# Router logits with the gate matrix as weights, and token rows of 320 columns

## The chip, the cores and the metric

The kernel runs on one core of a Trainium2 chip. The metric is the device time of one execution in microseconds (us), as the median of several runs. The core's engines are TensorE (PE, with its weight loads shown apart as PEld), VectorE (DVE), ScalarE (ACT), GpSimd (POOL) and SyncE (SP, which here only issues transfers).

## The reference

Three layers follow one another: a gated linear attention over 4 batches, 8 heads and 768 tokens, a router that gives each of the 3072 tokens to one of 8 experts with 384 tokens each, and a dense layer after the experts.

```python
def _moe_ref(x, w_gate, w1, w2):            # x: 3072 x 320, the attention's output
    logits = x @ w_gate                     # 320 x 8
    order = np.argsort(-logits.flatten())
    ...
    # in falling order: a token not yet placed goes to its expert while that has room (cap 384)
    for e in range(E):
        mask = assigned == e
        h = np.maximum(x[mask] @ w1[e], 0.0)    # 320 -> 1024
        out[mask] = h @ w2[e]                   # 1024 -> 320
    return out

def _moe2_ref(x, w_in, w_out):              # 320 -> 2048 -> 320
    h = x @ w_in
    g = np.where(h > 0.0, h, np.exp(np.minimum(h, 0.0)) - 1.0)
    return g @ w_out
```

## The kernel before

**Attention, about 0 to 168 us.** The work is cut into 24 units u: 12 blocks of 64 tokens by 2 pairs of batches, so that a unit has 128 tokens. `Attention.run` goes over the units. In one pass of its loop TensorE does, in this order: a zeroing matmul (L348), the values and scores (L357 and L289, 64x64 matmuls in f32), the decay matrices pD and pF (L314, L304, L307), the three transposes of the unit before (`turn(u-1)`, L428), recall and state (L371 and L384), and the logits of the unit before (L438). Meanwhile DVE divides and gates the unit's output into `x` (L404 to L411), POOL scales it (L412), ACT doubles its last 64 columns (L419) so that a row has 384 columns, and SP stores the rows to the scratch tensor `xd` in DRAM (L422). `turn` puts x^T into PSUM (`pX`), ACT copies it to `xT` (L430), and `logits` multiplies: xT is the weights (128 columns), and the 8 columns of the gate matrix `wg` move through it. ACT copies the 128x8 result to `L` (L439). Between the units, queues that were filled before (`at.extra`) give out other work: the first steps of the routing, four units at a time (`rt.early`, lines L610 to L630 on DVE), and the loading and splitting of weights (L872 to L938).

**Routing of the first expert, about 168 to 199 us.** A chain of small steps on DVE and TensorE selects the first 384 tokens.

**Eight rounds, about 199 to 768 us.** Each takes one expert's 384 tokens through the expert and then the dense layer. `get_x` gathers the rows of `xd` by indirect transfers of 128 rows each, issued by POOL (L996, tile `xg`). `prep_x` transposes them (`turn(k)`, three transposes for each of three tiles, L1061), and ACT and DVE split the result into two parts, xh and xl. The last 64 of the 320 columns are wanted twice, on partitions 0 to 63 and 64 to 127; in the kernel before the rows hold them twice. Then come the matmuls of the expert (L1108 with w1h, w1l; L1202 to L1217) and of the dense layer (L1108 with wih, wil; L1247 to L1251). Where the rounds' other work stands in TensorE's order is set by a planner with costs; the transposes of the next round stand among the dense layer's matmuls of the round before.

Of the kernel before, what the change touches and what calls it, by code (L numbers as in the profile page):

```python
# [8 lines left out]
F32 = mybir.dt.float32  # L9
# [3 lines left out]
AF = mybir.ActivationFunctionType  # L13
# [3 lines left out]
B, H, S, D = 4, 8, 768, 40  # L17
# [11 lines left out]
EP = [0, 1, 1, 1, 1, 1]  # L29
FU = 1  # L30
SPIN, IDLE, MX = 12, 1, [256, 512, 640]
NB, NL, PX = 2, 3, 0.2
WARM = [8, 2, 2, 2]

# [84 lines left out]
class Attention:  # L119
# [4 lines left out]
    def __init__(self, nc, tc, consts, qk, vk, ig, fg, wg, xd, L, ident):  # L124
        self.nc, self.tc, self.qk, self.vk, self.xd, self.L, self.ident = nc, tc, qk, vk, xd, L, ident
        self.es = ExitStack()
        one = self.es.enter_context(tc.tile_pool(name="a1", bufs=1))
        self.two = self.es.enter_context(tc.tile_pool(name="a2", bufs=2))
        self.psX = self.es.enter_context(tc.tile_pool(name="psX", bufs=1, space=PS))
        V, G, A = nc.vector, nc.gpsimd, nc.scalar  # L130
# [24 lines left out]
            self.load_vk(u)  # L155
        for u in range(2, 4):
            self.load_qk(u)
        self.wg = one.tile([128, 3, 8], F32, name="wg")
        nc.sync.dma_start(self.wg, wg)
        for u in range(2, 4):  # L160
            self.load_vk(u)
        m = one.tile([32, S + 1], F32, name="m")
        V.memset(m[:, 0:1], -1e30)
        keep = one.tile([32, S], F32, name="keep")
        G.memset(keep, 1.0)
        G.memset(keep[:, 0:S:64], 0.0)
        ac = one.tile([32, S], F32, name="ac")
# [27 lines left out]
        for x in self.KT:  # L195
            G.memset(x, 0.0)
        self.pC = self.psum("pC", 1)
        self.g = gi, gf, m, keep, ac

        t0, t1 = slice(0, 128), slice(128, S)  # L200
# [7 lines left out]
        self.decay(0)  # L208
        self.maximum(128, S)
        V.memset(self.pC, 0.0)  # L210
        self.decay(1)
        self.both(self.scores(1))
        self.weigh(0)
        self.fade(0)
        self.logs(2, NS)

    def psum(self, name, bufs):
        return self.psX.tile([128, 8, 64], F32, name=name, bufs=bufs)
# [180 lines left out]
    def gates(self, u, fl):  # L399

        V = self.nc.vector
        nq = self.st["O", u][:, :, 40]
        rd = self.two.tile([128, 2, 8], F32, name="rd")
        V.tensor_scalar(rd[:, 0], nq, -2.0, 2.0, op0=ALU.mult, op1=ALU.max)  # L404
        fl(1)
        V.scalar_tensor_tensor(rd[:, 0], nq, 2.0, rd[:, 0], op0=ALU.mult, op1=ALU.max)
        fl(5)
        V.reciprocal(rd[:, 1], rd[:, 0])
        x = self.st["x", u] = self.two.tile([128, 384], F32, name="x", bufs=3)
        xh = x[:, :320].rearrange("p (h d) -> p h d", d=40)  # L410
        V.scalar_tensor_tensor(xh, self.st.pop(("sg", u)), 1.0, self.st.pop(("O", u))[:, :, :40], op0=ALU.add, op1=ALU.mult)  # L411
        self.nc.gpsimd.tensor_tensor(xh, xh, rd[:, 1, :, None].to_broadcast([128, 8, 40]), op=ALU.mult)  # L412

    def rows_out(self, u):

        nc = self.nc
        n, bp = divmod(u, 2)
        x = self.st["x", u]
        nc.scalar.activation(x[:, 320:], x[:, 256:320], AF.Copy)  # L419
        for r in range(2):  # L420
            row = (bp * 2 + 1 - r) * S + n * 64
            nc.sync.dma_start(self.xd[row:row + 64], x[r * 64:r * 64 + 64])  # L422

    def turn(self, u):
        x = self.st.pop(("x", u))
        p = self.st["T", u] = self.psum("pX", 1).rearrange("p h t -> p (h t)")
        for k in range(3):
            self.nc.tensor.transpose(p[:, k * 128:k * 128 + 128], x[:, k * 128:k * 128 + 128], self.ident)  # L428
        xT = self.st["xT", u] = self.two.tile([128, 3, 128], F32, name="xT")
        self.nc.scalar.activation(xT.rearrange("p k t -> p (k t)"), p[:, :384], AF.Copy)  # L430

    def logits(self, u):

        l = self.st.pop(("T", u))[:, 384:392]
        x = self.st.pop(("xT", u))
        for k in range(3):
            z = 128 if k < 2 else 64
            self.nc.tensor.matmul(l, x[:z, k], self.wg[:z, k], start=k == 0, stop=k == 2)  # L438
        self.nc.scalar.activation(self.L[:, :, u % 4 * 6 + u // 4], l, AF.Copy)  # L439

    def step(self):

# [3 lines left out]
    def run(self, hook, fill):  # L446
        later = self.split(2, NS)
        for u in range(NU):
            v, w = u + 1, u + 2
            fl = lambda i: ([fill() for _ in range(FP[i])] if u > FU else []) + [self.step() for _ in range(EP[i])]  # L450
            self.idle(u)
            self.both(self.values(u), self.scores(w))
            if u < 3:
                next(later, None)
            if w < NU:
                self.decay(w)
            if u > 0:
                self.turn(u - 1)
            self.both(self.recall(u), self.state(u))
            if v < NU:  # L460
                self.factors(v)
                self.weigh(v)
            if u + 5 < NU:
                self.load_qk(u + 5)
            if v < NU:
                self.opens(v)
            fl(0)
            if v < NU:
                self.fade(v)
            self.gates(u, fl)  # L470
            fl(2)
            if u > 0:
                self.logits(u - 1)
            self.add_state(u)
            fl(3)
            if u == NU - 1:
                while self.extra:
                    self.step()
            self.rows_out(u)
            if u + 4 < NU:  # L480
                self.load_vk(u + 4)
            fl(4)
            hook(u)
        self.turn(u)
        self.logits(u)
        hook(NU)
        self.es.close()
# [336 lines left out]
class Mlp:  # L824
# [209 lines left out]
    def get_x(self, r):  # L1034
        idx = self.router.res[r][1]
        self.xg = []
        for k in range(3):
            t = self.pool.tile([128, 384], F32, name="xg", bufs=3)
            self.xg.append(t)
            self.gather(t, self.xd, idx[:, k:k + 1])  # L1040

# [10 lines left out]
    def prep_x(self, r):  # L1052

        nc, plan = self.nc, self.plan
        xh = self.pool.tile([128, 3, TK], F32R, name="xh", bufs=1)
        xl = self.pool.tile([128, 3, TK], F32R, name="xl", bufs=1)
        ps = []

        def turn(k):
            for t in range(3):  # L1060
                nc.tensor.transpose(ps[k][0][:, t * 128:t * 128 + 128], self.xg[k][:, t * 128:t * 128 + 128], self.ident)  # L1061

        def split(k):
            p, slot = ps[k]
# [17 lines left out]
        if r == 0:  # L1082
            ps = [self.psum() for t in range(3)]
# [336 lines left out]
def kernel(ctx, tc, qk, vk, ig, fg, wg, w1a, w1b, w2a, win, wout, out):  # L1420
    nc = tc.nc
# [4 lines left out]
    ident = consts.tile([128, 128], F32, name="ident")  # L1426
    make_identity(nc, ident)
    L = consts.tile([128, 8, 24], F32, name="L")
    xd = dram.tile([3072, 384], F32, name="xd")
    rt = Router.__new__(Router)  # L1430
    plan = Plan()
    m = Mlp(nc, tc, consts, w1a, w1b, w2a, win, wout, xd, out, ident, rt, plan)
# [13 lines left out]
    def hook(u):  # L1446
        if u in (0, 1):
            fill()
        if u == 2:
            at.extra.append(tables)  # L1450
        if 4 <= u < 23 and u % 4 == 0:
            at.extra.append(rt.early(u // 4 - 1))
        if u == 22:
            at.extra.append(rt.early(5, 0, 2))
        if u == 23:
            at.extra.append(rt.early(5, 2, 3))
        if u == 24:
            while at.extra:
                at.step()
            rt.dg = rt.digits(0)  # L1460
            for _ in rt.early(5, 3, 4, rt.dg):
                pass
# [9 lines left out]
    ps = ctx.enter_context(tc.tile_pool(name="ps", bufs=NPH, space=PS))  # L1472
# [8 lines left out]
def _layout(i):  # L1481
# [22 lines left out]
    d["ig"], d["fg"] = (i[n].reshape(2, 2, 8, 768).swapaxes(0, 1).reshape(32, 768) for n in ("i_gate", "f_gate"))  # L1504
    wg = i["moe_w_gate"][:, ::-1]
    d["wg"] = np.concatenate([wg, np.zeros((64, 8), wg.dtype)]).reshape(3, 128, 8).transpose(1, 0, 2)
    d["w1a"] = i["moe_w1"][:, :256].reshape(2048, 1024)
    d["w1b"] = i["moe_w1"][:, 256:].reshape(512, 1024)
    d["w2a"] = i["moe_w2"].reshape(8, 2, 4, 128, 320).transpose(0, 1, 3, 2, 4).reshape(2048, 1280)
# [20 lines left out]
```

## Time and profile before

| | us |
|---|---|
| time, median of 3 runs | 777.46 (776.14 to 778.16) |
| profiled execution | 777.53 |
| its span, first to last instruction | 775.5 |
| TensorE busy | 714.9 (92%) |
| VectorE busy | 543.0 (70%) |
| ScalarE busy | 383.0 (49%) |
| GpSimd busy | 214.5 (28%) |

The profile is of one execution. Its own time is 2.0 us longer than its span. A step of TensorE is best read from one start to the next, since matmuls are pipelined and the durations of neighbours overlap. The granted clock of TensorE is given as a share of full speed: 1.00 is 2.4 GHz, 0.50 is 1.2 GHz.

### The profile page before, as it was taken

To read this page: it belongs to the slowest core of one execution; us is meant where nothing else is said; L and a number is where in the kernel's file an instruction comes from. 1 tells how busy PE (TensorE), PEld (TensorE's weight loads), DVE (VectorE), ACT (ScalarE), POOL (GpSimd) and SP (SyncE) were. 2 spreads that over 40 slices of the span, in tenths; PEclk is the share of its full clock that TensorE was granted. 3 is DMA by queue.
4 is the path that set the end of the run, shared out by engine and by line. 5 is a ranking of instruction groups with operands and counts; after the bars stand their busy time and mean duration, and the time that the engine had idled before them with its cause. 6 is when DMAs were issued, how large, how long until landed. Compare 5 with 4: busy or idle time off the path is not lost.

```text
span 775.5 us, 18282 instructions
## 1 busy us (share of the span) xinstructions
PE 714.9 (92%) x7375; PEld 659.9 (85%) x7379; DVE 543.0 (70%) x1599; ACT 383.0 (49%) x817; POOL 214.5 (28%) x264
## 2 busy tenths in 40 slices
PE   7889787971899999999999999999999999999994
PEld 4767576861799998999999899999999999999994
DVE  8486787658878887885797589669868834842541
ACT  5655544433536644662575277246527734742541
POOL 5677767425411320301121031112023230001001
PEclk9699998685799999999999999999999999999998
DMA  7677967433500410310140032023003321100000
GB/s 256 193 227 214 247 198 215 138 94 94 181 8 1 146 61 2 118 64 27 26 156 19 9 102 79 26 83 99 1 26 108 130 77 39 35 1 27 0 1 26
DMA packets 22820, 68.86 MB, mean 89 GB/s; under 512 B 3536, under 2 KB 7632, under 8 KB 22736
## 3 DMA queue, kind: packets, MB, share of 16 engines
q1 hardware_dynamic: 14240, 35.87, 15.7%
q0 software_dynamic: 8448, 31.73, 12.6%
q8 instruction: 58, 0.95, 0.5%
q14 instruction: 26, 0.21, 0.1%
q10 hardware_dynamic: 48, 0.10, 0.0%
HBM read 59.03 MB, written 8.65 MB: 87 GB/s over the span
## 4 chain that ended last, share of the span: by engine, by line
PE 64%; issue 18%; DVE 8%; POOL 3%; ACT 3%; DMA 2%; SPq 0%; POOLq 0%; DVEq 0%; ACTq 0%
PE ph L1108 26%; PE acc L1247 5%; PE acc L1251 5%; PE acc L1248 5%; PE acc L1215 3%; PE acc L1217 2%; PE acc L1216 2%; PE pO L371 2%; PE pO L357 2%; PE pX L438 2%; DMA vk<-in_vk_dram 1%; PE acc L1202 1%; PE acc L1204 1%; PE pX L428 1%; DVE e L1161 1%
## 5 line engine op out<-in xcount | busy, mean ns | idle before, releaser
L1161 DVE SCALAR_TENSOR_TENSOR e<-e,ph 128x384 f32<-128x384 f32 x128 | 70.4, 550 | 54.7 <-ACT e L1158 54.1
L1157 ACT ACTIVATE e<-ph 128x384 f32<-128x384 f32 x128 | 62.4, 487 | 85.3 <-PE ph L1108 77.7
L1108 PE MATMUL ph<-yh,wih 128*128 128x384 f32 x256 | 89.9, 351 | 0.3
L1125 ACT ACTIVATE gh<-ph 128x384 fp32r<-128x384 f32 x64 | 31.4, 491 | 113.0 <-PE ph L1108 88.8
L1108 PE MATMUL ph<-yh,wil 128*128 128x384 f32 x256 | 86.6, 338 | 0.0
L1257 POOL DMA_INDIRECT out_dram<-ot,idx x24 | 24.1, 1004 | 210.1 <-ACT ot L985 207.1
L992 DVE TENSOR_TENSOR gl<-e,gh 128x384 fp32r<-128x384 f32 x128 | 71.0, 561 | 1.7 <-ACT gh L985 0.3
L1158 ACT ACTIVATE e<-e 128x384 f32<-128x384 f32 x128 | 67.3, 526 | 4.0
L1132 DVE SCALAR_TENSOR_TENSOR gl<-ph,gh 128x384 fp32r<-128x384 f32 x64 | 35.3, 554 | 46.9 <-ACT gh L1125 46.5
L1247 PE MATMUL acc<-woh,gh 128*128 128x320 f32 x216 | 68.1, 315 | 0.0
L1248 PE MATMUL acc<-wol,gh 128*128 128x320 f32 x216 | 66.7, 309 | 0.0
L1251 PE MATMUL acc<-woh,gl 128*128 128x320 f32 x216 | 66.7, 309 | 0.0
L1108 PE MATMUL ph<-yl,wih 128*128 128x384 f32 x256 | 66.6, 341 | 0.0
L996 POOL DMA_INDIRECT stg<-in_w1a_dram,wi x16 | 15.7, 982 | 148.6 <-DVE wi L765 134.2
L985 ACT ACTIVATE gh<-e 128x384 fp32r<-128x384 f32 x97 | 49.4, 514 | 11.1 <-DVE e L1161 10.8
L1251 PE MATMUL acc<-woa,gl 128*128 128x320 f32 x168 | 52.4, 312 | 0.8 <-DVE gl L992 0.8
L1247 PE MATMUL acc<-woa,gh 128*128 128x320 f32 x168 | 53.1, 316 | 0.0
L1248 PE MATMUL acc<-wob,gh 128*128 128x320 f32 x168 | 51.9, 309 | 0.0
L1108 PEld LDWEIGHTS ph<-yh,wih 128*128 128x128 f32 x256 | 48.2, 188 | 4.1 <-ACT yh L1220 4.1
L1108 PEld LDWEIGHTS ph<-yh,wil 128*128 128x128 f32 x256 | 48.1, 188 | 0.0
L1108 PEld LDWEIGHTS ph<-yl,wih 128*128 128x128 f32 x256 | 46.2, 188 | 0.0
L1108 PE MATMUL ph<-xh,w1h 128*128 128x384 f32 x128 | 44.9, 351 | 0.1
(269 smaller groups left out, 2118.2 us busy)
## 6 DMA issues: line engine op xcount, KB each, us to landing
vk<-in_vk_dram SPq DMA_DIRECT2D x24, 484.0 KB, 4.5
qk<-in_qk_dram SPq DMA_DIRECT2D x20, 320.0 KB, 5.3
xd<-x SPq DMA_DIRECT2D x48, 96.0 KB, 2.6
cx<-in_win_dram SPq DMA_DIRECT2D x8, 512.0 KB, 5.5
wx<-in_wout_dram SPq DMA_DIRECT2D x9, 320.0 KB, 3.1
cx<-in_wout_dram SPq DMA_DIRECT2D x5, 448.0 KB, 6.2
qk<-in_qk_dram SPq DMA_DIRECT2D x4, 512.0 KB, 7.2
cx<-in_win_dram SPq DMA_DIRECT2D x4, 256.0 KB, 7.4
```

The lines of the kernel that those rows point to most:

```text
L985: self.nc.scalar.activation(out, x, AF.Copy)
L992: self.nc.vector.tensor_tensor(out, x, y, op=ALU.subtract)
L1108: PE.matmul(p, w, x, start=k == 0, stop=k == 7)
L1125: nc.scalar.activation(h, p, AF.Relu)
L1132: nc.vector.scalar_tensor_tensor(l, p, 0.0, h, op0=ALU.max, op1=ALU.subtract)
L1157: nc.scalar.activation(e, p, AF.Relu, scale=-1.0)
L1158: nc.scalar.activation(e, e, AF.Exp, scale=-1.0)
L1161: nc.vector.scalar_tensor_tensor(e, e, -1.0, p, op0=ALU.add, op1=ALU.max)
L1247: PE.matmul(p, h[:, c], wh, start=f == 0, stop=False)
L1248: PE.matmul(p, h[:, c], wl, start=False, stop=False)
L1251: PE.matmul(p, l[:, c], wh, start=False, stop=f == 15)
L1257: s = nc.gpsimd.indirect_dma_start(out=self.out, out_offset=bass.IndirectOffsetOnAxis(ap=idx[:, t:t + 1], axis=0), in_=o, in_offset=None)
```

## The change

For units 0 to 19 (`TG = 20`) the logits change sides: the gate matrix, padded from 8 to 32 columns, is the weights, and the 128 columns of xT move. The result is 32 rows (8 of them used) by 128 tokens, and the four units of a group stand on the four quarters of the partitions of one PSUM tile. After four units one ACT copy takes that tile to `lT` in SBUF, and one unit later `tokens(g)` transposes it back on TensorE and copies 128x32 values into `L`. Units 20 to 23 keep the old form. `pX` is now one fixed PSUM tile that is zeroed once on DVE. `wg` lies in a part of the tile `keep` and is loaded after the scans that read `keep`. The early steps of the routing come one unit later (units 5, 9, ..., 21).

Rows of `x`, `xd` and `xg` have 320 columns, and ACT's copy of the last 64 is gone. In the attention the third transpose takes 64 columns. In the rounds the third transpose is replaced by two f32 matmuls with the 64 columns as weights and the identity moving, one to partitions 0 to 63 and one to 64 to 127.

```diff
+TG = 20
...
-        self.wg = one.tile([128, 3, 8], F32, name="wg")
-        nc.sync.dma_start(self.wg, wg)
...
-        keep = one.tile([32, S], F32, name="keep")
+        keep = keep_all = one.tile([128, S], F32, name="keep")
+        self.lT, keep = keep[:, :128], keep[:32]
+        self.wg = keep_all[:, 128:224].rearrange("p (k e) -> p k e", e=32)
...
+        self.pX = self.psum("pX", 1).rearrange("p h t -> p (h t)")
...
+        V.memset(self.pX, 0.0)
...
         self.logs(2, NS)
+        nc.sync.dma_start(self.wg, wg)
...
-        nc.scalar.activation(x[:, 320:], x[:, 256:320], AF.Copy)
...
-        p = self.st["T", u] = self.psum("pX", 1).rearrange("p h t -> p (h t)")
+        p = self.pX
         for k in range(3):
-            self.nc.tensor.transpose(p[:, k * 128:k * 128 + 128], x[:, k * 128:k * 128 + 128], self.ident)
+            z = 128 if k < 2 else 64
+            self.nc.tensor.transpose(p[:z, k * 128:k * 128 + 128], x[:, k * 128:k * 128 + z], self.ident)
...
     def logits(self, u):
-        l = self.st.pop(("T", u))[:, 384:392]
         x = self.st.pop(("xT", u))
+        b = u % 4 * 32
+        l = self.pX[:, 384:392] if u >= TG else self.pX[b:b + 32, 384:512]
         for k in range(3):
             z = 128 if k < 2 else 64
-            self.nc.tensor.matmul(l, x[:z, k], self.wg[:z, k], start=k == 0, stop=k == 2)
-        self.nc.scalar.activation(self.L[:, :, u % 4 * 6 + u // 4], l, AF.Copy)
+            if u >= TG:
+                self.nc.tensor.matmul(l, x[:z, k], self.wg[:z, k, :8], start=k == 0, stop=k == 2)
+            else:
+                self.nc.tensor.matmul(l, self.wg[:z, k], x[:z, k], start=k == 0, stop=k == 2)
+        if u >= TG:
+            self.nc.scalar.activation(self.L[:, :, u % 4 * 6 + u // 4], l, AF.Copy)
+        elif u % 4 == 3:
+            self.nc.scalar.activation(self.lT, self.pX[:, 384:512], AF.Copy)
+
+    def tokens(self, g):
+        p = self.pX[:, 384:512]
+        self.nc.tensor.transpose(p, self.lT, self.ident)
+        self.nc.scalar.activation(self.L[:, :, g::6], p.rearrange("p (b e) -> p e b", e=32)[:, :8], AF.Copy)
...
                 self.turn(u - 1)
+            if 5 <= u <= TG + 1 and u % 4 == 1:
+                self.tokens(u // 4 - 1)
             self.both(self.recall(u), self.state(u))
...
-            t = self.pool.tile([128, 384], F32, name="xg", bufs=3)
+            t = self.pool.tile([128, 320], F32, name="xg", bufs=3)
...
         def turn(k):
             for t in range(3):
-                nc.tensor.transpose(ps[k][0][:, t * 128:t * 128 + 128], self.xg[k][:, t * 128:t * 128 + 128], self.ident)
+                c = slice(t * 128, t * 128 + 128)
+                for q in (0, 64) if t == 2 else ():
+                    nc.tensor.matmul(ps[k][0][q:q + 64, c], self.xg[k][:, 256:], self.ident, start=True, stop=True)
+                if t < 2:
+                    nc.tensor.transpose(ps[k][0][:, c], self.xg[k][:, c], self.ident)
...
-    xd = dram.tile([3072, 384], F32, name="xd")
+    xd = dram.tile([3072, 320], F32, name="xd")
...
-        if 4 <= u < 23 and u % 4 == 0:
+        if 5 <= u <= TG + 1 and u % 4 == 1:
             at.extra.append(rt.early(u // 4 - 1))
```

ACT's program around the copies for units 0 and 1, before: fp, pb, db and W are the decay factors of a later unit, xT the transposed tokens, sg a gate.

```order
L419 ACTIVATE x<-x 128x64
L248 ACTIVATE fp<-ac 32x640
L249 ACTIVATE pb<-gi 32x640
L302 ACTIVATE db<-pD 128x512
L309 ACTIVATE W<-pF 128x512
L430 ACTIVATE xT<-pX 128x384
L337 ACTIVATE sg<-vk 128x320
L439 ACTIVATE L<-pX 128x8
L419 ACTIVATE x<-x 128x64
L248 ACTIVATE fp<-ac 32x640
```

The same place of ACT's program now (lines are those of the changed kernel).

```order
L252 ACTIVATE fp<-ac 32x640
L253 ACTIVATE pb<-gi 32x640
L306 ACTIVATE db<-pD 128x512
L313 ACTIVATE W<-pF 128x512
L434 ACTIVATE xT<-pX 128x384
L341 ACTIVATE sg<-vk 128x320
L252 ACTIVATE fp<-ac 32x640
```

The copies of x and of L are gone from between the factors; nothing else has moved there.

TensorE's program at the transposes of a later round, which stand among the dense layer's matmuls, before:

```order
L1251 MATMUL acc<-woh,gl 128x320
L1061 MATMUL ph<-ident,xg 128x128 x3
L1247 MATMUL acc<-woh,gh 128x320
L1248 MATMUL acc<-wol,gh 128x320
L1251 MATMUL acc<-woh,gl 128x320
L1061 MATMUL ph<-ident,xg 128x128 x3
L1247 MATMUL acc<-woh,gh 128x320
```

And now:

```order
L1273 MATMUL acc<-woh,gl 128x320
L1083 MATMUL ph<-ident,xg 128x128 x2
L1081 MATMUL ph<-ident,xg 64x128 x2
L1269 MATMUL acc<-woh,gh 128x320
L1270 MATMUL acc<-wol,gh 128x320
L1273 MATMUL acc<-woh,gl 128x320
L1083 MATMUL ph<-ident,xg 128x128 x2
L1081 MATMUL ph<-ident,xg 64x128 x2
L1269 MATMUL acc<-woh,gh 128x320
```

Two 64x128 matmuls stand where the third transpose stood, in 24 such places; the matmuls around them are the same. In the attention `tokens` adds one transpose on TensorE right after the three of `turn`, at units 5, 9, 13, 17 and 21.

## Rows read from the trace of the kernel before

**Rows 1.** Windows: from:to, length, busy us (count) by engine, granted clock, DMA share, GB/s.

```profile
25.00:38.00 13.00, 11.40 (x216) 9.44 (x209) 3.96 (x10) 7.70 (x15) 7.56 (x9) 0.50 0.64 195
...
86.00:89.00 3.00, 3.00 (x49) 2.18 (x45) 2.90 (x5) 1.61 (x4) 2.06 (x3) 0.50 1.06 220
...
134.00:147.00 13.00, 12.07 (x213) 9.63 (x216) 6.69 (x14) 5.45 (x13) 5.84 (x6) 0.50 0.58 164
...
202.00:768.00 566.00, 561.65 (x3675) 537.58 (x3673) 396.88 (x1218) 287.37 (x599) 90.16 (x113) 1.00 0.17 54
```

**Rows 2.** Waits of TensorE, 16 to 168 us: total us, times, longest.

```profile
PE pS L289 <- issue: 5.1, 4, 2.9
```

**Rows 3.** Timeline of TensorE, late units: start, duration, instruction, count [idle before <- releaser].

```profile
155.67 0.49 PE L428 MATMUL pX<-ident,x 128*128 128x128 f32 x3
156.09 0.27 PE L371 MATMUL pO<-C,qt 64*64 64x64 f32 x2
...
157.18 0.93 PE L438 MATMUL pX<-wg,xT 128*128 128x8 f32 x6
158.04 0.39 PE L348 MATMUL pO<-wz 128*128 128x512 bf16 x1
...
159.92 1.15 PE L371 MATMUL pO<-C,qt 64*64 64x64 f32 x32
161.00 0.93 PE L438 MATMUL pX<-wg,xT 128*128 128x8 f32 x6
```

**Rows 4.** Timeline of TensorE's weight loads at the same logits.

```profile
157.18 0.84 PEld L438 LDWEIGHTS pX<-wg,xT 128*128 128x128 f32 x6
```

**Rows 5.** Timeline of ACT in the first units.

```profile
19.89 0.26 ACT L419 ACTIVATE x<-x 128x64 f32<-128x64 f32 x1 [1.87 <-POOL x L412]
...
25.33 0.26 ACT L419 ACTIVATE x<-x 128x64 f32<-128x64 f32 x1 [1.10 <-POOL x L412]
```

**Rows 6.** Timeline of TensorE in the first units.

```profile
23.07 0.93 PE L438 MATMUL pX<-wg,xT 128*128 128x8 f32 x6 [1.15 <-ACT xT L430]
...
26.39 0.59 PE L314 MATMUL pD<-fp,sel 96*128 96x64 bf16 x8 [0.36 <-ACT fp L248]
...
28.61 0.61 PE L307 MATMUL pF<-one_m,fb 96*128 96x512 bf16 x1 [0.77 <-ACT fb L255]
29.01 0.85 PE L428 MATMUL pX<-ident,x 128*128 128x128 f32 x3
```

**Rows 7.** Transfers: issues, KB each, median us from issue to landing.

```profile
xg<-xd,idx POOLq DMA_INDIRECT x24, 3.1
...
wg<-in_wg_dram SPq DMA_DIRECT2D x1, 12.0 KB, 8.5
```

**Rows 8.** Timeline of DVE, the zeroing of a 128x512 PSUM tile, and a scan of `keep`.

```profile
9.14 0.48 DVE L210 MEMSET pC<- 128x512 f32 x1
...
12.35 1.48 DVE L237 TENSOR_TENSOR_SCAN ac<-keep,gf 32x640 f32<-32x640 f32 x1
```

**Rows 9.** Timeline of DVE, a last early step of the routing before the last unit.

```profile
166.52 0.54 DVE L630 TENSOR_TENSOR A<-w,a 128x16 bf16<-128x16 f32 x1
```

**Rows 10.** Timeline of TensorE at the transposes of a later round.

```profile
328.73 0.31 PE L1251 MATMUL acc<-woh,gl 128*128 128x320 f32 x1
328.88 0.49 PE L1061 MATMUL ph<-ident,xg 128*128 128x128 f32 x3
...
329.35 0.31 PE L1248 MATMUL acc<-wol,gh 128*128 128x320 f32 x1
329.50 0.31 PE L1251 MATMUL acc<-woh,gl 128*128 128x320 f32 x1
```

**Rows 11.** Timeline of TensorE in a round, a matmul with 64 weight columns among others.

```profile
357.87 0.34 PE L1202 MATMUL acc<-gl,w 128*64 128x384 f32 x1
358.04 0.34 PE L1204 MATMUL acc<-gh,w 128*128 128x384 f32 x1
```

**Rows 12.** Timeline of TensorE at the first round's tokens.

```profile
198.87 0.90 PE L1061 MATMUL ph<-ident,xg 128*128 128x128 f32 x3 [1.88 <-DMA xg<-xd,idx]
```

More of the change, by code (lines that the diff above doesn't have):

```diff
@@ L408, in gates @@
         V.reciprocal(rd[:, 1], rd[:, 0])
-        x = self.st["x", u] = self.two.tile([128, 384], F32, name="x", bufs=3)
+        x = self.st["x", u] = self.two.tile([128, 320], F32, name="x", bufs=3)
         xh = x[:, :320].rearrange("p (h d) -> p h d", d=40)
@@ L1506, in _layout @@
     d["wg"] = np.concatenate([wg, np.zeros((64, 8), wg.dtype)]).reshape(3, 128, 8).transpose(1, 0, 2)
+    d["wg"] = np.concatenate([d["wg"], np.zeros((128, 3, 24), wg.dtype)], 2)
     d["w1a"] = i["moe_w1"][:, :256].reshape(2048, 1024)
```

## The prediction

> **What bounds the kernel now.** The busy shares of the windows say that the kernel has two parts. From 202 us to the end TensorE is busy 561.65 of 566 us at full clock [rows 1]: there each step added to its program is a step added to the time, and nothing that other engines save is worth anything. In the attention TensorE also sets the pace, but with waits and with a clock that falls. The chain of work around a unit, read in the timeline, gives what a unit costs at full clock: the logits take from 157.18 to 158.04, 0.86 us; recall and state from 156.09 to 157.18, 1.09; three transposes from 155.67 to 156.09, 0.42 [rows 3]. Two things lengthen that. The first is waits: in the first units ACT holds TensorE up (1.15 us before the first logits, then 0.36 and 0.77 [rows 6]), and later the largest are waits for nothing that the profile shows, which I read as instructions not yet there (5.1 us on one line alone, up to 2.9 at once [rows 2]). The second is the clock. From 25 to 38 us and from 134 to 147 us it is granted at 0.50, 1.2 GHz, although TensorE works nearly all the time (11.40 and 12.07 of 13 us); other falls are short, as that of 86 to 89 us [rows 1]. The first long fall comes right behind the ACT waits of the first units.
>
> **The change, part by part.** Sums are made against the profiled execution, 777.53 us, which is 0.07 above the median of the runs, so the two may be taken as one.
>
> *ACT without its two copies.* L419 waits for POOL's x, at 19.89 us for 1.87 and at 25.33 for 1.10 us [rows 5], and the decay factors and xT queue behind it. TensorE's three waits [rows 6] hang on that queue: fp stands right behind L419, fb behind that, and xT behind W. Without the copies fp can start where ACT now idles. I take all of it: 1.15 + 0.36 + 0.77 = -2.3 us; bounds 0 (another wait takes their place) and -2.3. In later units such waits of ACT lie beside TensorE's work, and I count nothing.
>
> *Logits with 32 weight columns.* Six weight loads of 128 columns fill 0.84 of the 0.86 us [rows 4]: now the loading of xT sets the step, not the 8 moving columns. Turned round, 32 columns are loaded and 128 move. What 128 moving f32 columns cost in a matmul of two passes no row shows alone; a transpose moves the same 128 columns, and three take 0.33 us among other matmuls (below), 0.11 each. Six passes at that are 0.65; the old 0.86 holds about 0.2 more, for the third matmul with its 64 rows and the way back, and that may stay. So 0.65 to 0.86, and I take the middle, 0.75: 20 x -0.11 = -2.2 us (bounds -4.2 and 0).
>
> *`tokens`.* Five more transposes in the attention, a third of 0.42 each [rows 3]: +0.7 us. The copies that ACT adds (10) are fewer than the 44 it loses; hidden.
>
> *Start and end.* A second PSUM zeroing as that of 9.14 us takes DVE 0.48 us [rows 8], part of it beside its idle time: +0.2 (0 to 0.5). `wg` is loaded behind the scan that ends at 13.83 us [rows 8]; even with the 8.5 us that its load took in the crowded start [rows 7] it lands at about 22.4, before the logits that now start at 23.07, and about 0.5 us late for logits that start 1.15 earlier. A 3.1 us landing [rows 7] hides it, and I count nothing. The routing steps that come one unit later put one more DVE operation of up to 0.54 us [rows 9] ahead of the last unit's x: +0.2 (0 to 0.5).
>
> *Transposes in rounds 1 to 7.* From L1251 at 328.73 to L1248 at 329.35 is 0.62 us with three transposes in it; without them it is two steps of 0.15 (329.35 to 329.50), so three cost 0.33 us [rows 10]. Now two remain, 0.22, and two f32 matmuls of two passes follow, 0.22 us each if alone. Can they run beside each other, on two halves of the columns? The nearest row says yes: in f32 with 64x64 pieces, 32 recall matmuls alone take 159.92 to 161.00, 1.08 us, and 32 recall together with 32 state matmuls (one after the other in pairs) take the same 1.09 [rows 3]. So the pair costs 0.22 to 0.43. A change of form may cost more: the third step of the logits does. But a 64-column matmul among 128-column ones is followed by the next after 0.17 us, though the step has 384 columns [rows 11]. I take 0.22 and 0.08 for one change of form: 0.52 in place of 0.33, +0.19 each, 21 times, +4.0 us; bounds +0.11 (+2.3) and +0.33 (+6.9). The Trainium skill says that a change of the tiling mode drains TensorE, and that tiles work independently (TensorEngine Tiling (Array Packing), Key Properties). The rows agree with the second; for the first, rows 11 shows none for columns that start at partition 0, and nothing in this trace shows columns at 64 behind a full-width matmul. By that rule the pair pays on the way in and on the way back; what this would give is among the rivals.
>
> *Round 0.* The clock is at 0.50 there, all steps double: 3 x 0.38 = +1.1. The gather is waited for (1.88 us [rows 12]) and moves a sixth less of its 3.1 us [rows 7]: -0.2 (0 to -0.5).
>
> Without the clock this makes -2.3 - 2.2 + 0.7 + 0.2 + 0.2 + 4.0 + 0.9 = +1.5 us.
>
> *The clock.* At 0.50 three transposes last 0.85 us, at full clock 0.49 [rows 3, 6]: work done at the low clock takes 1.7 times as long, and 0.42 of a low stretch is lost. The low stretch from 25 us on begins after TensorE waited for ACT, and it stays although TensorE is then busy. The change takes away the waits ahead of it, and replaces the logits within it. If that stretch ends as soon as the short one (3 us, 86 to 89), 10 of its 13 us or a little more leave the low clock, and 10.3 x 0.42 = -4.3 us. I count this as the likeliest, since both what came before the stretch and a part of what fills it change; no row shows that it must. The stretch from 134 us comes behind a long wait for instructions, which the change does not touch; I leave it.
>
> Sum: 777.5 + 1.5 - 4.3 = 774.7 us.
>
> **The rivals.** *The low stretch stays* (chance 0.25). For it: TensorE was busy for 0.88 of it and the clock did not rise, and most of its work stays the same. Then +1.5 stands alone: 779.0, or 777.0 with the logits at 0.65 (-4.2 in place of -2.2). *Both long stretches shorten* (0.17). The second holds the same logits, and TensorE was busy 12.07 of its 13 us. Another -4.3: 770.4. *The pair runs serially, or pays for its form twice* (0.13). Against it are the 64x64 rows, for it that those pieces lie on other rows of the array as well, which these do not. Serial it costs +0.33 each in place of +0.19, 2.9 us over the rounds and 0.8 in round 0: 778.4 with the shortened stretch, 782.7 without. With 0.1 for each of two changes of form (the 0.2 of the logits) it costs +0.31 each, nearly the same: 777.9 and 782.2. The rule of the Trainium skill on the drain (same page and section) speaks for this second way. *Slower by the clock* (0.10): the waits for instructions are as they were but fall elsewhere, and one more of the short falls becomes a long one. That decides from 10 us of low clock on, +4.3 on top of +1.5: 783.3. *The change does not do what it says* can be only for ACT: if POOL's x, which the transposes need anyway, sets TensorE's waits, 2.3 us of the gain are missing; this lies in the range.
>
> **How the numbers follow.** The forecast, that the first long stretch shortens, has 0.35, with its own range of 772 to 777.5 (logits from 0.65 to 0.86, -2.0 to +2.2, and the pair from +0.11, -1.7). 0.3% is 2.3 us, about what a measurement here can tell from no change: faster means under 775.1, slower over 779.8. Faster: 0.23 of the forecast's 0.35, all of the 0.17, and 0.05 of the stretch that stays, with fast logits: 0.45. Slower: 0.09 of the serial pair, all of the 0.10, and 0.09 of the stretch that stays: 0.28. The same: 0.27. The range leaves out the best part of the two-stretch case and the worst of the slow ones: 768.5 to 782.
>
> **What would show it.** In the trace after: the three waits of the first units gone; the logits' six steps at 0.75 us at full clock; from L1251 over the two transposes and the pair to the second matmul behind them 0.81 us, not 0.62, and the two matmuls of the pair starting together; the clock from 25 to 38 us at 1.00 for most of it. The prediction is wrong if the clock stays low there, if the pair's matmuls start 0.2 us apart, or if a wait for `wg` stands before the first logits.

## The result, and the profile after

The changed kernel takes 780.37 us (median of 19 runs, 777.49 to 784.86). Measured beside it, the kernel before takes 772.5 us (19 runs, 767.57 to 778.16), so the three runs shown ahead lie at the upper end of what it does. The ratio of the two is 1.0098, 95% interval 1.0077 to 1.0119: the change costs 7.6 us by the ratio. The forecast was a gain of 2.8 us. All ratios in this document compare the fast runs of both kernels, and leave out the few executions in a slower state.

The profiled execution of the changed kernel took 778.76 us, with a span of 777.0. The windows of that execution, as in [rows 1]:

```profile
25.00:38.00 13.00, 12.07 (x394) 9.01 (x394) 6.92 (x19) 7.01 (x14) 8.54 (x9) 1.00 0.79 250
...
86.00:89.00 3.00, 2.35 (x23) 1.09 (x26) 2.56 (x8) 1.30 (x2) 1.27 (x1) 0.71 1.04 268
...
134.00:147.00 13.00, 11.49 (x359) 8.19 (x358) 11.22 (x23) 7.75 (x17) 9.13 (x9) 1.00 0.45 125
...
202.00:768.00 566.00, 563.97 (x3700) 533.68 (x3698) 390.99 (x1203) 283.26 (x589) 87.87 (x111) 1.00 0.15 50
```

Both long stretches at 0.50 are gone from these windows: TensorE runs at 1.00 where it ran at half before. Whether the change did this, two single executions cannot say; e3 comes back to it. The first tokens of round 0 come much earlier than in [rows 12]. TensorE's timeline there, in the changed kernel:

```profile
189.44 0.53 PE L1083 MATMUL ph<-ident,xg 128*128 128x128 f32 x2 [2.35 <-DMA xg<-xd,idx]
189.90 0.70 PE L1081 MATMUL ph<-ident,xg 128*64 128x128 f32 x4
```

So the attention and the first routing took 189.4 us in place of 198.9, 9.4 us less in these two executions, of which the one before had an uncommonly low clock (below). From there to the end of the span it is 777.0 - 189.4 = 587.6 us, and before it was 775.5 - 198.9 = 576.6: the rounds take 11.0 us more. The pair of f32 matmuls is where most of them go. TensorE's timeline in a round of the changed kernel, to be set beside [rows 10]:

```profile
262.18 0.31 PE L1273 MATMUL acc<-woh,gl 128*128 128x320 f32 x1
262.33 0.38 PE L1083 MATMUL ph<-ident,xg 128*128 128x128 f32 x2
262.64 0.44 PE L1081 MATMUL ph<-ident,xg 128*64 128x128 f32 x4
263.01 0.41 PE L1269 MATMUL acc<-woh,gh 128*128 128x320 f32 x1
263.26 0.31 PE L1270 MATMUL acc<-wol,gh 128*128 128x320 f32 x1
```

From L1273 to the second matmul behind it is now 263.26 - 262.18 = 1.08 us; it was 0.62. Each place costs 0.46 us more. Of the 1.08 us two plain steps are 0.30 and two transposes 0.22, so the pair has 0.56, where the third transpose had 0.10. Two transposes take 0.22, so the pair starts about 0.1 late (262.64 and not 262.55), and the next matmul starts 0.37 us behind it. The step behind that is 0.25 long; that alone is no mark of the pair, since behind transposes it is 0.23 (e1 and e9 below). TensorE's weight loads at the same place:

```profile
262.64 0.20 PEld L1081 LDWEIGHTS ph<-ident,xg 128*64 128x64 f32 x4 [0.17 <-issue]
263.01 0.19 PEld L1269 LDWEIGHTS acc<-woh,gh 128*128 128x128 f32 x1 [0.17 <-issue]
```

No weights are loaded for 0.17 us ahead of the pair, and again for 0.17 us ahead of the matmul behind it. 21 such places make 9.7 us. The rest, 1.3 us, is a difference only: in it are round 0's three places and how much of round 0 fell to the low clock, which these runs do not separate.

The logits at full clock, in TensorE's timeline of the changed kernel, beside [rows 3]:

```profile
141.55 0.96 PE L446 MATMUL pX<-xT,keep 128*32 128x128 f32 x6
142.44 0.39 PE L352 MATMUL pO<-wz 128*128 128x512 bf16 x1
```

They take 0.89 us, where the old ones took 0.86: slightly more than before. At unit 5, where `tokens` comes in for the first time, TensorE and then ACT of the changed kernel:

```profile
45.36 0.49 PE L432 MATMUL pX<-ident,x 128*128 128x128 f32 x3
46.80 0.33 PE L454 MATMUL pX<-ident,keep 128*128 128x128 f32 x1 [0.94 <-ACT xT L434]
47.05 0.27 PE L375 MATMUL pO<-C,qt 64*64 64x64 f32 x2
```

```profile
46.25 0.50 ACT L434 ACTIVATE xT<-pX 128x384 f32<-128x384 f32 x1
47.16 0.23 ACT L455 ACTIVATE L<-pX 128x32 f32<-128x32 f32 x1 [0.42 <-PE pX L454]
```

The transpose of `tokens` waits until ACT has copied the transposes of the unit just turned. They lie in other columns of the same tile pX, and I read the shared tile as the reason; e4, where the wait is gone, agrees. Recall starts 1.69 us behind the first transpose, where it was 0.42 [rows 3]. The waits of TensorE from 16 to 157 us show all five (first two columns: total and times):

```profile
PE pC L388 <- issue: 6.7, 3, 3.5
PE pX L454 <- ACT xT L434: 3.8, 5, 0.9
...
PE pX L446 <- ACT xT L434: 2.0, 2, 1.6
```

### The profile page after: what moved, and what is told of

It is laid out like the page before. It is cut to its first block, busy times and chain, and to the rows that moved or that the text cites. A ratio compares the mean times of both kernels' runs of the same rounds, so it can differ in the third digit from the quotient of the medians.

```text
span 777.0 us, 18383 instructions
## 1 busy us (share of the span) xinstructions
PE 715.7 (92%) x7456; PEld 645.0 (83%) x7456; DVE 546.0 (70%) x1600; ACT 377.4 (49%) x783; POOL 216.0 (28%) x264
## 4 chain that ended last, share of the span: by engine, by line
PE 58%; issue 19%; POOL 10%; DMA 5%; DVE 4%; ACT 1%; SPq 1%; POOLq 0%; ACTq 0%; DVEq 0%
PE ph L1130 28%; PE acc L1269 6%; PE acc L1273 5%; PE acc L1270 5%; POOL qt L325 3%; DMA qk<-in_qk_dram 3%; PE acc L1237 3%; PE acc L1238 2%; PE acc L1239 2%; POOL kt L334 2%; POOL C L336 1%; DMA vk<-in_vk_dram 1%; PE acc L1224 1%; POOL x L416 1%; PE ph L1081 1%
## 5 line engine op out<-in xcount | busy, mean ns | idle before, releaser
L1273 PE MATMUL acc<-woh,gl 128*128 128x320 f32 x216 | 66.7, 309 | 0.0
L1273 PE MATMUL acc<-woa,gl 128*128 128x320 f32 x168 | 52.4, 312 | 0.8 <-DVE gl L1010 0.8
```

What stands on the lines that cost most here:

```text
L1273: PE.matmul(p, l[:, c], wh, start=False, stop=f == 15)
```

## The experiments

The first theory after the result: the rounds lose 11 us by the pair alone, by its form and not by its columns; the attention gains by the clock and by ACT's missing copies, and loses part of it to `tokens`. The rivals: the rounds grew by the rows of 320 columns; the clock has nothing to do with the new logits.

### Another way to double the columns (e1)

```diff
-                for q in (0, 64) if t == 2 else ():
-                    nc.tensor.matmul(ps[k][0][q:q + 64, c], self.xg[k][:, 256:], self.ident, start=True, stop=True)
-                if t < 2:
+                if t == 2:
+                    nc.tensor.transpose(ps[k][0][:, c], self.xg[k][:, 192:], self.ident)
+                    nc.tensor.transpose(ps[k][0][:64, c], self.xg[k][:, 256:], self.ident)
+                else:
```

The first of the two transposes puts columns 256 to 319 onto partitions 64 to 127, the second onto 0 to 63, over columns that nobody wants there.

> The pair of f32 matmuls in the rounds is replaced by two transposes: one of columns 192 to 319 (full width), then one of columns 256 to 319 onto partitions 0 to 63. Theory (the pair costs by its form: it drains TensorE on the way in and out, 0.93 us from the first transpose to the second matmul behind, where three transposes took 0.48): four transposes take 0.11 us more than three, not 0.455 more, so some 0.34 us of each of 21 places and 1.5 us of round 0 come back, 8.7 us in all; ratio to the kernel before 0.997 to 1.001. Rival (the rounds grew because the rows of 320 columns are stored and gathered otherwise, not by the pair): the time stays as in the changed kernel, ratio 1.007 or more.

Measured: 773.55 us (12 runs), ratio 1.0027 (0.9999 to 1.0055), a little above the range expected and below the rival's. From round 0's first transposes to the end it is 578.7 us, 8.9 less than in the changed kernel; the ratios give back 5.5, with an uncertainty of some 3. TensorE's timeline in a round:

```profile
263.02 0.31 PE L1274 MATMUL acc<-woh,gl 128*128 128x320 f32 x1
263.17 0.38 PE L1084 MATMUL ph<-ident,xg 128*128 128x128 f32 x2
263.39 0.27 PE L1081 MATMUL ph<-ident,xg 128*128 128x128 f32 x1
263.50 0.27 PE L1082 MATMUL ph<-ident,xg 128*64 128x128 f32 x1
263.52 0.39 PE L1270 MATMUL acc<-woh,gh 128*128 128x320 f32 x1
263.75 0.31 PE L1271 MATMUL acc<-wol,gh 128*128 128x320 f32 x1
```

A transpose of 64 columns takes its 0.11 us like a full one: 0.73 us over the place (263.02 to 263.75), 0.11 more than before. The rows of 320 columns stayed, so they are not the cause. But the doubling is cheap here, and the kernel is still not faster than before: what the attention was to gain is missing too.

### The rows and rounds of before (e2)

Here `x`, `xg` and `xd` have 384 columns again, ACT copies the last 64, and the rounds have three transposes; the logits and `tokens` are the new ones.

> The rounds and the rows are as before (384 columns, ACT's copy of the last 64 in each unit, three transposes); only the logits with tokens are the new ones. Theory that the pair is the loss: 11.7 us of the rounds come back (0.455 x 21 and 2.1 in round 0), and ACT's copy costs at most 2.3 us again: ratio 0.994 to 0.999. The theory of the prediction (the rounds lose 4.9 us, the attention gains) gives 1.002 to 1.006.

Measured: 774.27 us (12 runs), ratio 1.0016 (0.9991 to 1.0041). The rounds were back to 576.7 us from round 0's first transposes to the end of the span, all 11 us. The ratio lies above the range that the theory gave, at the edge of what the theory of the prediction gave. In this form the attention shows no gain, within some 2 us: the new logits and `tokens`, with ACT's copies, are worth nothing together.

### The logits of before in all units (e3)

```diff
-TG = 20
+TG = 0
...
-        if 5 <= u <= TG + 1 and u % 4 == 1:
+        if 4 <= u < 23 and u % 4 == 0:
             at.extra.append(rt.early(u // 4 - 1))
```

> TG = 0: all units have the logits of before (xT as weights, 8 columns move), without tokens, with the early steps of the routing at units 4 to 20 as before; rows of 320 columns and the pair stay. Theory that the new logits keep the clock up: the attention has the low stretches of before again, ratio 1.008 or more. Rival that they only cost (0.03 us for each unit, and 1.25 us for each of five tokens, which wait for the copy of xT): 6.8 us come off, ratio 1.000 to 1.003, the attention's clock as high as in the changed kernel, since ACT's copies are gone there too.

Measured: 779.45 us (6 runs), ratio 1.0108 (1.0064 to 1.0152). The mean granted clock over its runs is 0.957, over those of the changed kernel 0.962. By the intervals this says that the logits do not give back 6.8 us when they are undone: what they cost is matched by what they bring, to within some 4 us. The rival fell. Its profiled execution, with the logits of before, has these windows:

```profile
25.00:38.00 13.00, 11.31 (x369) 9.20 (x359) 6.72 (x18) 8.08 (x17) 7.93 (x9) 1.00 0.75 240
134.00:147.00 13.00, 12.80 (x429) 10.46 (x425) 9.66 (x19) 7.58 (x17) 9.43 (x9) 1.00 0.43 119
```

Both are at 1.00 here as well, and round 0's first transposes come at 188.2 us, earlier than in the changed kernel (189.4). So the long stretches of the one profile before are no work of the old logits by themselves, and that they are missing after the change does not show what the change did.

### `tokens` at another place (e4)

```diff
             self.both(self.values(u), self.scores(w))
+            if 5 <= u <= TG + 1 and u % 4 == 1:
+                self.tokens(u // 4 - 1)
...
             if u > 0:
                 self.turn(u - 1)
-            if 5 <= u <= TG + 1 and u % 4 == 1:
-                self.tokens(u // 4 - 1)
```

> Only the place of tokens is changed: behind the values and scores of its unit in place of behind the transposes of turn. Theory: the transpose of tokens waits about 1 us for ACT's copy of xT, since both lie in one PSUM tile; here nothing reads that tile, so 5 x 1 us come off, ratio 1.003 to 1.005. Rival: TensorE waits for that unit's other inputs anyway and the place does not matter, ratio 1.008 to 1.011.

Measured: 778.88 us (12 runs), ratio 1.0077 (1.0046 to 1.0107), beside 1.0098 (1.0077 to 1.0119) for the changed kernel: a gain of some 1.6 us that these intervals do not separate from nothing. e12 and e2, below and above, differ by the place of `tokens` alone too: 0.9978 and 1.0016, 2.9 us, with intervals that overlap. Both pairs point the same way. The wait itself is gone; of the waits of TensorE in e4 from 16 to 157 us the largest are now:

```profile
PE pC L388 <- issue: 10.0, 4, 4.0
PE pO L361 <- DVE P L346: 3.0, 1, 3.0
PE pS L293 <- issue: 2.7, 2, 2.4
PE pX L446 <- issue: 2.6, 2, 1.8
```

L454 waits for nothing, but the first line, a wait for nothing that the profile shows, has grown from 6.7 to 10.0 us. That part of the wait taken away comes back there is possible, but not shown: the same line has 7.0 us in e9 and 5.0 in e12, which have `tokens` at this place too.

### Old logits with the cheap doubling, and GpSimd's copy (e5, e6, e10)

e5 joins e1 and e3. e6 has the logits of before too, but in rounds 1 to 7 GpSimd copies the columns behind the gather, and three transposes follow as before:

```diff
-            self.gather(t, self.xd, idx[:, k:k + 1])
+            self.gather(t[:, :320], self.xd, idx[:, k:k + 1])
+        for t in self.xg if r else ():
+            self.nc.gpsimd.tensor_copy(t[:, 320:], t[:, 256:320])
```

> The logits of before in all units, no tokens, rows of 320 columns, no copies of x on ACT, and in the rounds two transposes (columns 192 to 319, then 256 to 319 onto partitions 0 to 63) in place of the pair. Against the kernel before, the attention differs by ACT's missing copies and by the rows alone. Theory that these are the change's whole gain (about 3 us) and that the cheap doubling costs 2.0 us: ratio 0.996 to 1.000. Theory that the new logits bring the gain through the clock: the attention is as before, ratio 1.002 to 1.005.

Measured: 773.14 us (12 runs), ratio 1.0022 (0.9993 to 1.0052): ACT's missing copies and the narrower rows, without the new logits, were not seen to pay for the cheap doubling. e1 is this kernel with the new logits and `tokens`, and its ratio is the same (1.0027): as with e3 and the changed kernel, the new logits with `tokens` in that place bring no time.

> As the run with the logits of before and the two transposes, but in rounds 1 to 7 GpSimd copies the last 64 columns behind the gather and three transposes follow, as in the kernel before; round 0 keeps the two transposes. Theory: GpSimd is idle there, the rounds take 566.6 us plus at most 0.5 in round 0, the attention keeps its gain: ratio 0.993 to 0.997. Rival: GpSimd waits for the gather with the weights' gathers queued behind it, and TensorE waits for weights: rounds of 568 us or more.

Measured: 773.07 us (12 runs), ratio 0.9998 (0.9971 to 1.0025). The rounds are as before (577.0 us from the first transposes to the end), so GpSimd's copies are hidden; the attention's gain that I expected is missing. The expectations of e6 to e11 count the rounds from the first matmul into `acc`, at 208.90 us in the kernel before, to the end; there it is 566.6 us before and 566.5 in e6. e6 was run again beside e9:

> The kernel with the logits of before and GpSimd's copy once more, on the same chip as the one with the new logits, for the two to be compared: ratio to the kernel before 0.998 to 1.002, mean clock near 0.954.

Measured: 771.41 us (12 runs), ratio 0.9975 (0.9953 to 0.9996), just below the range expected; mean clock 0.953. e6 and e10 are one kernel on two chips, and their ratios lie 1.8 us apart: differences of that size between chips say little here.

### What makes the pair dear (e7, e8, e11)

Three kernels, with one run each, for the place in the rounds. In e7 one f32 matmul of full width stands in the pair's place (its lower rows hold other columns); in e8 three transposes and one f32 matmul of 64 columns onto partitions 0 to 63; in e11 two transposes, one of 64 columns onto 0 to 63, and one f32 matmul of 64 columns onto 64 to 127.

> In place of the pair one f32 matmul with columns 192 to 319 as weights: full width, two passes, no half. The lower 64 rows of the result hold columns 192 to 255 in place of 256 to 319, so the expert's third part is computed from other values. Theory that the pair pays for its form: here two passes of 0.11 us without a drain, 0.11 to 0.15 us more than three transposes, from the first transpose to the second matmul behind about 0.6 us, rounds near 569.5 us. Rival that f32 matmuls with their two passes are slow behind transposes whatever their width: 0.8 us or more, rounds of 575 us and more.

> Three full transposes (the third of columns 192 to 319), then one f32 matmul with the 64 columns onto partitions 0 to 63 alone; the result is that of the changed kernel. Theory that a half of the columns drains TensorE whichever half it is, in f32: about 0.2 us in, two passes, 0.2 us out, 0.5 us more than three transposes, rounds near 578 us. Rival that only the half at partition 64 makes the drain (a 64-column matmul at partition 0 ran without one in the kernel before): two passes of 0.11 us, 0.25 us more than three transposes, rounds near 572 us.

> In the rounds a transpose of the 64 columns onto partitions 0 to 63, then one f32 matmul of the 64 columns onto partitions 64 to 127. Theory that an f32 matmul with 64 weight columns changes TensorE's form and drains it: the same extra time as with the one f32 matmul on partitions 0 to 63, less a transpose: about 0.93 us from the first transpose to the second matmul behind, the same as the pair, rounds 577 us. Rival that two halves beside each other are what is slow: 0.7 us or less.

TensorE's timeline in a round of e7, of e8 and of e11:

```profile
265.81 0.31 PE L1273 MATMUL acc<-woh,gl 128*128 128x320 f32 x1
265.96 0.38 PE L1083 MATMUL ph<-ident,xg 128*128 128x128 f32 x2
266.18 0.39 PE L1081 MATMUL ph<-ident,xg 128*128 128x128 f32 x2
266.32 0.39 PE L1269 MATMUL acc<-woh,gh 128*128 128x320 f32 x1
266.55 0.31 PE L1270 MATMUL acc<-wol,gh 128*128 128x320 f32 x1
```

```profile
265.13 0.27 PE L1081 MATMUL ph<-ident,xg 128*128 128x128 f32 x1
265.34 0.43 PE L1082 MATMUL ph<-ident,xg 128*64 128x128 f32 x2
265.70 0.41 PE L1270 MATMUL acc<-woh,gh 128*128 128x320 f32 x1
265.95 0.31 PE L1271 MATMUL acc<-wol,gh 128*128 128x320 f32 x1
```

```profile
264.23 0.38 PE L1084 MATMUL ph<-ident,xg 128*128 128x128 f32 x2
264.44 0.27 PE L1081 MATMUL ph<-ident,xg 128*64 128x128 f32 x1
264.65 0.43 PE L1082 MATMUL ph<-ident,xg 128*64 128x128 f32 x2
265.01 0.41 PE L1270 MATMUL acc<-woh,gh 128*128 128x320 f32 x1
265.26 0.31 PE L1271 MATMUL acc<-wol,gh 128*128 128x320 f32 x1
```

In e7 the place takes 0.74 us (265.81 to 266.55), as long as in e1: two passes of the full width have 0.22 us of it (0.74 less 0.30 for two plain steps and 0.22 for two transposes), as much as two transposes. In e8 one f32 matmul of half the width starts 0.21 us behind the transpose, the next matmul 0.36 us behind it, and the step behind is 0.25 long; in e11, on the other half, the numbers are the same (0.21, 0.36, 0.25). The whole place is 1.18 us in both, with three transposes in it (264.77 to 265.95 in e8), so 0.55 is left for the one matmul. In the changed kernel the pair of both halves takes 0.37. So the two halves do run beside each other, as the prediction took it, at no cost for the second. The weight loads of e7:

```profile
266.07 0.30 PEld L1081 LDWEIGHTS ph<-ident,xg 128*128 128x128 f32 x2
266.29 0.19 PEld L1269 LDWEIGHTS acc<-woh,gh 128*128 128x128 f32 x1
```

They start 0.11 us ahead of their matmul (266.07 and 266.18), and there is no gap before them; those of the pair start with their matmul, behind a gap. The place of the pair is 0.34 us longer than that of e7 (1.08 and 0.74). What costs is that an f32 matmul with 64 weight columns stands there at all, whichever half it goes to; a transpose of 64 columns (e1) and the 64-column matmul of [rows 11] do not have this cost. The latter has operands of type fp32r in the kernel's text (the profile writes f32) and one pass; which of the two spares it the cost was not tested. The expectations of e7 and e8 came out: 0.59 us from e7's first transpose to the second matmul behind, and rounds of 568.8 and 577.4 us. That of e11 was 0.1 too low, 1.03 us (264.23 to 265.26) and not 0.93, since the transpose of 64 columns that stands there too takes 0.11; its rounds are 577.3. e7 came to 775.96 us, e8 to 783.63 and e11 to 782.85, one run each.

### The gains without the losses (e9, e12)

e9 is the changed kernel with `tokens` behind the values and scores, GpSimd's copy in rounds 1 to 7 and the two transposes in round 0. e12 is e2 with `tokens` at that place: rows and rounds of before, ACT's copies too.

> The new logits with tokens behind the values and scores, rows of 320 columns, and in rounds 1 to 7 GpSimd's copy with three transposes (round 0: two transposes). Theory: the new logits cut the time at the low clock by some 12 us (mean over the runs so far: 57 to 59 us with them, 67 to 72 without), worth 5 us, and cost 2 to 4 us more work; with the rounds as cheap as before the ratio is 0.992 to 0.997. Rival: the gain in clock and the added work cancel, ratio 0.998 to 1.002, the same as with the logits of before.

Measured: 767.58 us (6 runs), ratio 0.9935 (0.9911 to 0.9959): faster than before by 5.0 us, and than the changed kernel by some 12.6 by the ratios. Beside e10, on the same chip and with the logits of before, it is 3.1 us faster by the ratios, and the two intervals just overlap. TensorE in a round of e9:

```profile
261.52 0.31 PE L1276 MATMUL acc<-woh,gl 128*128 128x320 f32 x1
261.68 0.49 PE L1083 MATMUL ph<-ident,xg 128*128 128x128 f32 x3
261.92 0.39 PE L1272 MATMUL acc<-woh,gh 128*128 128x320 f32 x1
262.15 0.32 PE L1273 MATMUL acc<-wol,gh 128*128 128x320 f32 x1
```

The place takes 0.63 us, as before.

> As the kernel before in rows and rounds (384 columns, ACT's copy of the last 64 in each unit, three transposes in the rounds), with the new logits and with tokens behind the values and scores. It differs from the fastest kernel so far (ratio 0.9935) by ACT's copies in the attention, the rows' width and round 0. Theory that ACT's copies cost 1 to 2.3 us in the attention: ratio 0.995 to 0.998. Rival that they cost nothing: 0.992 to 0.994.

Measured: 769.79 us (12 runs), ratio 0.9978 (0.9948 to 1.0007). That lies in the theory's range and outside the rival's. Against e9 it is 3.3 us of ratio for ACT's copies, the wider rows and round 0, on another chip and with intervals that overlap.

## Why the prediction was wrong

Two parts of the sum failed. The rounds were to lose 4.9 us and lost 11.0; the attention was to gain 7.7 (ACT, logits, `tokens`, start and end, clock) and gained an estimated 3.4, which is the 11.0 of the two profiles less the 7.6 of the ratio. Had the rounds lost only the 4.9, the change would still have been slower, by some 1.5 us; and e1, where the doubling is cheap, is not faster than before. The measured 780.37 us lies within the stated range of 768.5 to 782, but the forecast inside it was a gain.

*Transposes in rounds 1 to 7* is the term that missed most: +0.19 us for a place, measured +0.46, so +9.7 us in place of +4.0. The working asked the right question and answered half of it. That the two halves run beside each other held. That a change of form costs 0.08 did not: the pair takes 0.56 us of the place, and a full-width f32 matmul 0.22 (e7), so the form costs 0.34. About 0.1 of that is on the way in; the rest lies from the start of the pair on, with a second gap of 0.17 us in the weight loads behind it. [Rows 11], on which I leaned, is a matmul of another kind (fp32r, one pass). The rule of the Trainium skill that I cited, that a change of the tiling mode drains TensorE (TensorEngine Tiling (Array Packing), Key Properties), agrees with the gaps on both sides of the pair. I gave the case in which the pair runs serially or pays for its form twice a chance of 0.13, and priced the second at +0.31, still too low.

*ACT without its two copies*: the three waits of the first units are gone, as forecast. But the first logits do not start 1.15 us earlier. Nothing holds them behind recall and state, and yet they start at 23.70, where it was 23.07 [rows 6]:

```profile
22.62 1.15 PE L388 MATMUL pC<-vk,kt 64*64 64x64 f32 x32
23.70 0.96 PE L446 MATMUL pX<-xT,keep 128*32 128x128 f32 x6
```

Two things further ahead have grown: a wait for DVE (L361 for P) from 1.4 to 2.6 us, and a short fall of the clock, which was 0.81 from 16 to 25 us and 0.97 there before. The gain is seen one unit later, beside e2, which has the new logits and still ACT's copies (and 0.81 from 16 to 25 us as well). TensorE's timeline in the changed kernel, and then in e2:

```profile
26.91 0.49 PE L432 MATMUL pX<-ident,x 128*128 128x128 f32 x3
```

```profile
29.07 0.39 PE L311 MATMUL pF<-one_m,fb 96*128 96x512 bf16 x1 [1.36 <-ACT fb L259]
29.30 0.50 PE L433 MATMUL pX<-ident,x 128*128 128x128 f32 x3
```

Without the copies the transposes come 2.4 us earlier; the forecast was 2.3. What of this lasts to the end is only bounded: e9 and e12 differ by 3.3 us, e10 shows up to 1.9, e5 and e6 none.

*Logits with 32 weight columns*: forecast -2.2, measured +0.03 x 20 = +0.6 us. The bound was wrong on that side: the moving columns cost as much as the weights cost before, and the extra steps for the third matmul stayed.

*`tokens`*: forecast +0.7 for the transposes. I costed the instruction and not its wait: five waits of up to 0.9 us for the copy of xT, 3.8 in all. Moving `tokens` gave 1.6 and 2.9 us (e4; e12 beside e2), neither clear of nothing. The diff showed that ACT reads pX between the transposes of `turn` and `tokens`; I did not ask what TensorE would wait for there.

*Round 0*, and *start and end*: no wait for `wg` stands before the first logits, as taken. The other terms were not measured one by one.

*The clock*: the size came out near the forecast, but not by the mechanism that the prediction gave, so that is luck. It said that the first long stretch ends early because the waits of ACT ahead of it go and the logits in it change. The two long stretches of 0.50 are missing in e3 too, with the logits of before; and none of the 13 profiled executions after the change or in an experiment has a stretch of more than 7 us at 0.50 ahead of the first routing. What the change does to the clock is seen only in the mean over many runs. It is 0.954 for the kernel before (81 runs), 0.953 to 0.957 for the kernels with the logits of before (e3, e5, e6, e10), and 0.962 to 0.964 for all with the new logits (the changed kernel, e1, e2, e4, e9, e12), whatever else they had. A difference of 0.008 in a span of 771 us is 2 x 0.008 x 771 = 12 us less at the low clock; by the prediction's 0.42 that is an estimated 5 us, and the forecast said 4.3. So what lifts the clock comes with the new logits, and not with ACT's missing copies of x: e3, e5, e6 and e10 have no such copies either, and e2 and e12 have them. Within one chip it is 0.963 beside 0.957 (e1, e2 and e4 beside e3) and 0.964 beside 0.953 (e9 beside e10). New logits here means the six passes with 128 moving columns in place of 8, and with them `tokens`, fewer copies of L on ACT and the later routing steps; these were not taken apart, and why the clock answers is not shown by these runs. Nor does the lift show as time wherever it is: e3 and the changed kernel, and e5 and e1, differ by it and have the same ratios within their intervals.

One more thing misled: the profile of before, with a mean clock of 0.945, was of an execution with more low clock than most, 5 us above the median of the later runs. Of those 81 runs, 77 had a higher clock. The forecast of 774.7 us took away from 777.5 a stretch that need not be there at that length.

Of the prediction's own signs of being wrong none came: the clock from 25 to 38 us is high, the two halves run beside each other, and there is no wait for `wg`. They asked whether the halves run together, and not what they cost. Among the times that it named for the trace after, two did fail: 1.08 us for the place and not 0.81, and 0.89 for the logits and not 0.75.

In sum, of the 7.6 us: the rounds lost 11.0, and the attention gained 3.4: an estimated 5 by the clock and what ACT's copies gave, less `tokens`, the logits and waits that came back elsewhere. How these share it stays open.

## What to carry to other kernels

Before a small f32 matmul goes into a dense stream on TensorE, its form must be priced and not only its columns: with 64 weight columns among full-width ones it cost about 0.56 us, as a pair or alone, while a full-width f32 matmul cost 0.22 and a transpose of the same columns 0.11. Read what a place costs from a plain step ahead of it to a plain step behind it, since the start of a single step can shift without changing the whole. A free engine may do the same more cheaply: GpSimd's 21 copies of 0.25 us cost the rounds nothing that could be seen. When a tile gets a second use, ask of each instruction that touches it which copy it will wait for. And before a forecast is built on a stretch of a profile, see in a second execution whether it is there.

## What the runs showed of the hardware

In the rounds an f32 transpose takes 0.11 us whether it has 64 or 128 columns of weights (the place grows from 0.62 to 0.73 us with one of 64 more, e1). An f32 matmul of 128 weight columns and 128 moving ones takes 0.22 there (e7). With 64 weight columns it takes about 0.56, on either half (e8, e11), and the two halves together take no more than one (1.08 us for the place of the pair); no weights are loaded for 0.17 us on both sides of it. With the logits of 32 weight columns and 128 moving ones in 20 units of the attention, and what came with them, the mean granted clock was 0.962 to 0.964 where it was 0.953 to 0.957 with the old ones, though these logits took 0.03 us longer.
